# Retention and two MLP layers: the first 256-token units of the first layer begin one pair later, and the last unit follows the last pair

## The chip, the cores and the metric

The kernel runs on one core of one Trainium2 chip. The metric is the device time of one execution in microseconds (us), lower is better.

## What is computed

The reference makes a retention layer (attention without softmax, with a decay by distance) for 4 batches, 8 heads, 576 tokens and 64 values per head, and sends its 2304 tokens of 512 values through two layers with 2048 hidden values each.

```python
rel = pos[:, None] - pos[None, :]
Dmat = np.where(rel >= 0, gamma[:, None, None] ** rel[None, :, :], 0.0)
ret = scores * Dmat[None, :, :, :]          # scores = q k^T / 8
x = np.matmul(ret, v)                        # heads side by side: 2304 x 512
h = x @ w_in;  x = np.maximum(0.01 * h, h) @ w_out      # first layer
h = x @ w_in2; x = (h - np.tanh(h)) @ w_out2            # second layer
```

## The kernel before

**Precision.** Products that must be precise are made of three TensorE matmuls each, on a high and a low part of both factors (`xh`, `xl`, and the two halves of each `w` slot). The weights come as 64-bit floats. Each piece (128 x 512) is narrowed and split on the chip in these steps: a load (L147, issued on SyncE's queue, SP), `begin` on ScalarE (L164), `clamp` (L170), `shift` (L175), `top` and `low` (both L181) on VectorE, and a split into its two parts, ScalarE (L253) and then GpSimd (L254).

**Pairs.** The retention goes through 16 pairs (batch, two heads), numbered 0 to 15 here. Iteration `i` of the loop loads pair `i + 2`, makes the scores of pair `i` on TensorE (L674), has GpSimd scale its q (L642, and the last 64 tokens in L652), has VectorE mask the scores (L697, L708), and then calls `pair_steps(i)`: the outputs of pair `i - 1` on TensorE (L755, L766), the states of pair `i` (L723 on TensorE, L731 on ScalarE, L733 on VectorE), and the result of pair `i - 1`, split into `xh` (L774, ScalarE) and `xl` (L775, VectorE). The loads of a pair are four transfers on SP (L627, L628, L634, L635). The `kv` tiles have three buffers, so the transfer L634 of pair `i + 2` waits until the outputs of pair `i - 1` have been read, and what stands behind it on SP waits too.

**Units.** From pair `first` on, each pair also holds a share of the first layer, a unit of 256 tokens and two of the first four hidden blocks; there are 12, numbered 0 to 11. `unit_h(u)` is 24 matmuls into the one PSUM tile `x_b` (L822), then two activations on ScalarE that read it and write it (L828, L829), and a subtraction on VectorE that reads it (L830). Only after L830 may the next unit write `x_b`. `unit_o(u)` is 48 matmuls (L847) and stands one pair after `unit_h(u)`; `unit_evac` brings its sum out (L864, L866, L867). Units 0 and 1 need pieces 0 and 1 in `unit_h` and pieces 2 and 3 in `unit_o`; units 2 and 3 need pieces 4 and 5, and then 6 and 7.

**The narrowing steps.** All steps of the pieces stand in one list, and `fill(i, part)` issues it up to an index, at three places in each pair: part 0 ahead of `unit_h`, part 1 behind it, part 2 at the pair's end. The index is that of the table `early`, or else a third of the way between two `marks`. Pieces 0 to 7 take steps 0 to 52. Steps 53 and 54 are the loads of the first two of eight *kept* pieces (output weights of the second layer, `in_w2o`), steps 55 and 56 are `begin` and `clamp` of the first one, steps 57 and 58 its `shift` and `top`. The pieces are loaded into unused columns of `acc`, in four places: a load also waits until the piece that lay there has been narrowed. From pair 9 on the index comes from `marks` alone: 57 for (9, 0), 59 for (9, 1), 62 for (9, 2).

All engines work through their instructions in the order in which the program issues them, and each waits for what it needs. After the retention the function `layers` goes on with the rest of both layers.

Of the kernel before, what the change touches and what calls it, by code (L numbers as in the profile page):

```python
# [35 lines left out]
def retention_moe_moe(  # L36
# [15 lines left out]
    B, NP, _, S = qT.shape  # L52
# [26 lines left out]
    def slot(k, lead):  # L79
        at = k * 1024 + (LEAD if lead else 0)  # L80
        return wide_all[:, at:at + 1024].rearrange("p (i c) -> p i c", i=2)
# [25 lines left out]
    for m in range(2):  # L107
        for g in range(NG):
# [13 lines left out]
            first = len(steps)  # L122
# [438 lines left out]
    def retention():  # L561
        with ExitStack() as ac:
# [208 lines left out]
            def finish(i, src, lo, hi):  # L771
# [13 lines left out]
            marks = [0] + at_pair + [  # L785
                base + 2 + (len(ops) - base - 2) * i // (len(order) - 8) for i in range(len(order) - 7)
            ]
            first = NP + 1
            done, u = [0], 0

            early = {
# [3 lines left out]
            }  # L795

            def fill(i, part):
# [11 lines left out]
            def place(u):  # L809
                half, block = u % 2, u // 2  # L810
                if u < SPLIT:
                    half, block = block, half
                return block * QW, half * 2

            def unit_h(u):
                t0, f0 = place(u)
                for f in range(2):
                    w = wt[0, 0, f0 + f]
                    for kk in range(KK):
                        cs = slice(kk * P, (kk + 1) * P)  # L820
                        for j, (wi, x) in enumerate(((0, xh), (0, xl), (1, xh))):
                            nc.tensor.matmul(  # L822
                                out=x_b[:, f, :], lhsT=w[:, wi, cs], rhs=x[:, kk, t0:t0 + QW],
                                start=f == 0 and kk == 0 and j == 0,
                                stop=f == 1 and kk == KK - 1 and j == 2, skip_group_check=True,
                            )
                gt = slot(N_OUT + u % 2, True).rearrange("p i (f n) -> p i f n", f=2)
                nc.scalar.activation(out=gt[:, 0], in_=x_b, func=AF.Prelu, alpha=0.01)  # L828
                nc.scalar.activation(out=x_b, in_=x_b, func=AF.Prelu, alpha=0.01)  # L829
                nc.vector.tensor_tensor(  # L830
                    out=gt[:, 1], in0=x_b, in1=gt[:, 0].bitcast(F32), op=ALU.subtract
                )
                gs[u] = gt

            def unit_o(u):
                t0, f0 = place(u)
                gt = gs.pop(u)
                alone = u < SPLIT
                if alone or f0 == 0:
                    accs[t0] = ps_a.tile([P, KK, QW], F32, tag="a", name="a")  # L840
                ps = accs[t0]
                for f in range(2):
                    w = wt[0, 1, f0 + f]
                    for d in range(KK):
                        for j, (wi, gi) in enumerate(((0, 0), (0, 1), (1, 0))):

                            nc.tensor.matmul(  # L847
                                out=ps[:, d, :], lhsT=w[:, wi, d * P:(d + 1) * P],
                                rhs=gt[:, gi, f, :],
                                start=(alone or f0 == 0) and f == 0 and j == 0 and d % 2 == 0,  # L850
                                stop=(alone or f0 > 0) and f == 1 and j == 2 and d % 2 == 1,
                                skip_group_check=True,
                            )

            def unit_evac(u):
                t0, f0 = place(u)
                if f0 == 0 and u >= SPLIT:
                    return
                ps = accs.pop(t0)
                dst = acc_t[:, :, t0:t0 + QW]  # L860
                if f0 and u < SPLIT:
                    for d in (0, 2):
                        part = dst[:, d:d + 2]
                        nc.vector.tensor_tensor(out=part, in0=ps[:, d:d + 2], in1=part, op=ALU.add)  # L864
                    return
                nc.scalar.activation(out=dst[:, 2:], in_=ps[:, 2:], func=AF.Copy)  # L866
                nc.vector.tensor_copy(out=dst[:, :2], in_=ps[:, :2])  # L867

            def pair_steps(i, fast):

                nonlocal u
                if fast:
                    unit_h(u)
                    fill(i, 1)
                    if u:
                        unit_o(u - 1)
                        unit_evac(u - 1)
                    u += 1
                if i:
                    ot = o_place(i - 1)  # L880
                    if i < GROUPED:
                        outputs_far(i - 1, ot, range(1, NFULL))
                        outputs_near(i - 1, ot, range(NFULL))
                        outputs_far(i - 1, ot, [NFULL])
                        outputs_near(i - 1, ot, [NFULL])
                    else:
                        outputs_far(i - 1, ot, range(1, NCH))
                        outputs_near(i - 1, ot, range(NCH))
                        finish(i - 1, ot[:, :MAIN], 0, MAIN)
                    del qk[i - 1]  # L890
                    del pts[i - 1], kv[i - 1]
                if i < len(order):
                    states_mm(i)
                    scores_tail(i)
                    states(i)
                if i:
                    finish(i - 1, x_t, MAIN, S)
                    if i < GROUPED:
                        finish(i - 1, ot[:, :MAIN], 0, MAIN)
                if i < len(order):  # L900
                    mask_tail(i)
                if i + 1 < GROUPED:
                    prep_tail(i + 1)
                if i + 1 < len(order):
                    prep_k(i + 1)
# [57 lines left out]
                    fill(i, 2)  # L963
            pair_steps(len(order), True)
            assert done[0] >= len(ops)
            unit_o(u - 1)
            unit_evac(u - 1)
            assert 2 * u == n_early
# [168 lines left out]
    with tc.manual_schedule():  # L1137
        retention()
        layers()
# [70 lines left out]
```

## Time and profile before

| | |
|---|---|
| median of 3 runs | 858.77 us (858.19 to 858.89) |
| profiled execution | 858.63 us |
| its span, first to last instruction | 856.7 us, so 1.93 us lie outside it |
| TensorE (PE) busy | 847.5 us (99%) |
| VectorE (DVE) busy | 608.5 us (71%) |
| ScalarE (ACT) busy | 445.7 us (52%) |
| GpSimd (POOL) busy | 377.7 us (44%) |

The span is the time from the first instruction to the last. A busy share says how long an engine had an instruction in work, and not whether the program waited for that engine; that is told by the waits and by the chain that ended last. PEld is TensorE's weight load. A name ending in q (SPq) is an engine's queue, its issuing side.

### The profile page before, as it was taken

To read this page: it belongs to the slowest core of one execution; us is meant where nothing else is said; L and a number is where in the kernel's file an instruction comes from. 1 tells how busy PE (TensorE), PEld (TensorE's weight loads), DVE (VectorE), ACT (ScalarE), POOL (GpSimd) and SP (SyncE) were. 2 spreads that over 40 slices of the span, in tenths; PEclk is the share of its full clock that TensorE was granted. 3 is DMA by queue.
4 is the path that set the end of the run, shared out by engine and by line. 5 is a ranking of instruction groups with operands and counts; after the bars stand their busy time and mean duration, and the time that the engine had idled before them with its cause. 6 is when DMAs were issued, how large, how long until landed. Compare 5 with 4: busy or idle time off the path is not lost.

```text
span 856.7 us, 15321 instructions
## 1 busy us (share of the span) xinstructions
PE 847.5 (99%) x5774; PEld 751.4 (88%) x5774; DVE 608.5 (71%) x1052; ACT 445.7 (52%) x879; POOL 377.7 (44%) x308
## 2 busy tenths in 40 slices
PE   9999999999999999999999999999999999999997
PEld 8889999888988888888888899888999899999996
DVE  7987875787675777658764687756766677677775
ACT  4453443453345334453544577765566566656663
POOL 4432322140146103363465487745445445544554
PEclk9999999999999999999999999999999999999999
DMA  9835755334365433645354512581225312563112
GB/s 346 320 121 186 240 158 189 103 110 137 124 219 204 143 123 103 241 177 158 158 199 151 192 63 86 173 343 74 75 99 205 140 74 75 204 238 124 50 50 73
DMA packets 37784, 133.77 MB, mean 156 GB/s; under 512 B 4304, under 2 KB 4944, under 8 KB 35664
## 3 DMA queue, kind: packets, MB, share of 16 engines
q1 hardware_dynamic: 37424, 132.66, 43.7%
q8 instruction: 45, 0.74, 0.3%
q14 instruction: 27, 0.22, 0.1%
q10 hardware_dynamic: 288, 0.15, 0.1%
HBM read 96.62 MB, written 36.18 MB: 155 GB/s over the span
## 4 chain that ended last, share of the span: by engine, by line
PE 93%; DVE 4%; issue 1%; ACT 1%; POOL 0%; DVEq 0%; POOLq 0%
PE a L426 41%; PE h L273 22%; PE h L307 18%; PE a L847 4%; PE x_b L822 3%; PE o L766 1%; PE sc L674 1%; DVE cw L181 1%; PE o L755 1%; PE x_c L723 1%; PE x_b L942 1%; DVE st L733 0%; DVE pt L697 0%; DVE xl L775 0%; PE x_e L687 0%
## 5 line engine op out<-in xcount | busy, mean ns | idle before, releaser
L426 PE MATMUL a<-w 128*128 128x512 f32 (+1 forms) x1680 | 394.3, 377 | 0.0
L426 PEld LDWEIGHTS a<-w 128*128 128x128 f32 x1680 | 293.4, 188 | 47.5
L254 POOL TENSOR_TENSOR w<-cw,w 128x512 fp32r<-128x512 f32 x80 | 113.6, 1438 | 240.1 <-ACT w L253 214.4
L273 PE MATMUL h<-xh,w 128*128 128x512 f32 (+1 forms) x672 | 186.9, 349 | 0.0
L366 POOL TENSOR_TENSOR v<-t,u 128x512 f32<-128x512 f32 (+1 forms) x76 | 93.5, 1230 | 98.2 <-ACT t L363 92.2
L273 PEld LDWEIGHTS h<-xh,w 128*128 128x128 f32 x672 | 119.4, 188 | 17.0
L398 POOL TENSOR_TENSOR w<-v,w 128x512 fp32r<-128x512 f32 (+1 forms) x76 | 96.3, 1267 | 62.2 <-ACT w L397 62.1
L352 ACT ACTIVATE w<-h 128x512 fp32r<-128x512 f32 (+1 forms) x68 | 37.2, 547 | 159.9 <-PE h L273 115.7
L273 PE MATMUL h<-xl,w 128*128 128x512 f32 (+1 forms) x336 | 117.0, 348 | 0.0
L307 PE MATMUL h<-xh,w 128*128 128x256 f32 x512 | 100.8, 281 | 0.2
L307 PEld LDWEIGHTS h<-xe,w 128*128 128x128 f32 x576 | 80.9, 189 | 9.5 <-DVE mk L301 1.8
L181 DVE SCALAR_TENSOR_TENSOR cw<-st,cw 128x512 uint32<-128x512 uint32 x96 | 86.5, 901 | 2.5
L392 DVE SCALAR_TENSOR_TENSOR v<-q,v 128x512 f32<-128x512 f32 (+1 forms) x76 | 61.9, 814 | 36.5 <-POOL v L366 35.4
L307 PEld LDWEIGHTS h<-xh,w 128*128 128x128 f32 x512 | 83.1, 190 | 2.8 <-DVE v L395 1.5
L307 PE MATMUL h<-xe,w 128*128 128x256 f32 x576 | 84.2, 282 | 0.4 <-DVE mk L301 0.4
L511 DVE TENSOR_TENSOR acc<-a,acc 128x512 f32<-128x512 f32 (+1 forms) x113 | 71.3, 657 | 17.0 <-PE a L426 17.0
L362 ACT ACTIVATE u<-h 128x512 f32<-128x512 f32 (+1 forms) x80 | 44.2, 553 | 73.5 <-DVE h L301 51.3
L397 ACT ACTIVATE w<-v 128x512 fp32r<-128x512 f32 (+1 forms) x76 | 45.3, 596 | 62.5 <-DVE v L395 60.0
L170 DVE TENSOR_SCALAR cw<-cw 128x512 f32<-128x512 f32 x64 | 33.6, 525 | 55.6 <-ACT cw L164 55.4
L307 PE MATMUL h<-xl,w 128*128 128x256 f32 x256 | 71.8, 280 | 0.0
L273 PEld LDWEIGHTS h<-xl,w 128*128 128x128 f32 x336 | 63.3, 188 | 8.6
L253 ACT ACTIVATE w<-cw 128x512 fp32r<-128x512 f32 x80 | 47.0, 621 | 31.6 <-DVE cw L181 17.8
(95 smaller groups left out, 1178.4 us busy)
## 6 DMA issues: line engine op xcount, KB each, us to landing
kept<-w SPq DMA_DIRECT2D x48, 512.0 KB, 3.4
w<-kept SPq DMA_DIRECT2D x48, 512.0 KB, 4.7
xe<-xkept SPq DMA_DIRECT2D x12, 1536.0 KB, 6.5
st<-in_w2i SPq DMA_DIRECT2D x16, 512.0 KB, 4.1
st<-in_w1i SPq DMA_DIRECT2D x12, 512.0 KB, 4.4
st<-in_w1o SPq DMA_DIRECT2D x12, 512.0 KB, 3.5
xkept<-xe SPq DMA_DIRECT2D x4, 1536.0 KB, 8.8
kv<-in_vn SPq DMA_DIRECT2D x16, 320.0 KB, 3.3
```

What stands on the lines that cost most here:

```text
L181: nc.vector.scalar_tensor_tensor(out=t["w"], in0=t[src], scalar=scalar, in1=t["w"], op0=op, op1=ALU.bitwise_or)
L253: nc.scalar.activation(out=wp[:, 0, :], in_=wf, func=AF.Copy)
L254: nc.gpsimd.tensor_tensor(out=wp[:, 1, :], in0=wf, in1=wp[:, 0, :].bitcast(F32), op=ALU.subtract)
L273: nc.tensor.matmul(out=ps[:, :n], lhsT=w[:, wi, cs], rhs=x[:, kk, t0:t0 + n], start=kk == 0 and i == 0, stop=kk == KK - 1 and i == 2,)
L307: nc.tensor.matmul(out=out_, lhsT=w[:, wi_, at:at + P], rhs=x(xi, kk), start=start and kk == 0 and j == 0, stop=stop and kk == 1 and j == ...
L362: nc.scalar.activation(out=u[:, :n], in_=h, func=AF.Square)
L366: nc.gpsimd.tensor_tensor(out=v[:, :n], in0=t_[:, :n], in1=u[:, :n], op=ALU.mult)
L392: nc.vector.scalar_tensor_tensor(out=v, in0=q, scalar=RHO_A, in1=v, op0=ALU.add, op1=ALU.mult)
L397: nc.scalar.activation(out=gt[:, 0, g_at(s)], in_=v, func=AF.Copy)
L398: (nc.gpsimd if m else nc.vector).tensor_tensor(out=gt[:, 1, g_at(s)], in0=v, in1=gt[:, 0, g_at(s)].bitcast(F32), op=ALU.subtract)
L426: nc.tensor.matmul(out=o, lhsT=l, rhs=r, start=f == 0 and i == 0 and d % pack == 0, stop=f == GF - 1 and i == 2 and (d + 1) % pack == 0, s ...
L511: nc.vector.tensor_tensor(out=dst, in0=a, in1=dst, op=ALU.add)
```

## The change

The first unit stands in pair 6 instead of pair 5 (`first = NP + 2`, with `NP` = 4). Eleven units then stand in pairs 6 to 15 and in the closing `pair_steps`, and the twelfth is written behind them: `unit_h(11)`, `unit_o(10)`, and then `unit_o(11)` as before. The table `early` has the steps 0 to 52 one pair later from pair 4 on, with other places in between.

```diff
-            first = NP + 1
+            first = NP + 2
             done, u = [0], 0
 
             early = {
-                (1, 0): 3, (2, 0): 6, (2, 2): 7, (3, 0): 11, (4, 0): 12, (4, 2): 20,
-                (5, 0): 24, (5, 1): 30, (5, 2): 34, (6, 0): 38, (6, 1): 44, (6, 2): 47,
-                (7, 0): 50, (7, 1): 51, (7, 2): 53,
+                (1, 0): 3, (2, 0): 6, (2, 2): 7, (3, 0): 11, (4, 0): 12, (4, 2): 14,
+                (5, 0): 17, (6, 0): 20, (6, 1): 27, (6, 2): 31, (7, 0): 34, (7, 1): 40,
+                (7, 2): 44, (8, 0): 46, (8, 1): 50, (8, 2): 53,
             }
...
             pair_steps(len(order), True)
             assert done[0] >= len(ops)
+            unit_h(u)
+            unit_o(u - 1)
+            unit_evac(u - 1)
+            u += 1
             unit_o(u - 1)
             unit_evac(u - 1)
```

On VectorE, from the mask of pair 5 on, the order before has piece 2 narrowed ahead of that mask (L170, L175 and two L181, then L697), and unit 0's subtraction (L830) behind the first half of piece 3:

```order
L170 TENSOR_SCALAR cw<-cw 128x512
L175 TENSOR_SCALAR cw<-cw 128x512
L181 SCALAR_TENSOR_TENSOR cw<-acc,cw 128x512 x2
L697 TENSOR_TENSOR pt_97<-sc,cm_sb 128x512 x2
L170 TENSOR_SCALAR cw<-cw 128x512
L175 TENSOR_SCALAR cw<-cw 128x512
L830 TENSOR_TENSOR w<-x_b,w 128x512
L181 SCALAR_TENSOR_TENSOR cw<-acc,cw 128x512 x2
```

In the change, from the same place, the mask of pair 5 comes first, the rest of pair 5 and the mask of pair 6 stand inside piece 2, and unit 0's subtraction stands behind piece 2:

```order
L697 TENSOR_TENSOR pt_97<-sc,cm_sb 128x512 x2
L170 TENSOR_SCALAR cw<-cw 128x512
L175 TENSOR_SCALAR cw<-cw 128x512
L775 TENSOR_TENSOR xl<-o,xh 128x512
L733 SCALAR_TENSOR_TENSOR st_94<-st_94,decay,x_c 128x64 x3
L775 TENSOR_TENSOR xl<-x_e,xh 128x64
L708 TENSOR_TENSOR pt_97<-x_e,cm_sb 64x64
L708 TENSOR_TENSOR pt_97<-x_c,cm_sb 64x64
L697 TENSOR_TENSOR pt_96<-sc,cm_sb 128x512 x2
L181 SCALAR_TENSOR_TENSOR cw<-acc,cw 128x512 x2
L830 TENSOR_TENSOR w<-x_b,w 128x512
```

So a whole pair's work on VectorE has moved ahead of each piece from piece 2 on, beside the one unit that stands a pair later.

On SP, a piece of the difference shows the loads of the first kept pieces (`in_w2o`). Before, two of them stand behind the loads of pair 10 and ahead of those of pair 11; in the change the loads of pair 11 come first, and three stand together behind them:

```order
-L147 DMA acc<-in_w2o 128x512 x2
+L147 DMA acc<-in_w1o 128x512
 L627 DMA qk<-in_qT 128x576
 L628 DMA qk<-in_kT 128x576
 L634 DMA kv<-in_kn 128x512
 L635 DMA kv<-in_vn 128x640
-L147 DMA acc<-in_w2o 128x512
+L627 DMA qk<-in_qT 128x576
+L628 DMA qk<-in_kT 128x576
+L634 DMA kv<-in_kn 128x512
+L635 DMA kv<-in_vn 128x640
+L147 DMA acc<-in_w2o 128x512 x3
```

The two loads have moved behind one more L634, that of pair 11, from pair 8 into pair 9.

On ScalarE, the order before has `begin` of the first kept piece (the L164 of these rows) in pair 9, behind the activations of unit 3 and ahead of those of unit 4:

```order
L828 ACTIVATE w<-x_b 128x512
L829 ACTIVATE x_b<-x_b 128x512
L774 ACTIVATE xh<-o 128x512
L731 ACTIVATE st_93<-x_c 128x64
L774 ACTIVATE xh<-x_e 128x64
L658 ACTIVATE kv<-kv,acc 128x4x64 x2
L164 ACTIVATE cw<-acc 128x512
L828 ACTIVATE w<-x_b 128x512
L829 ACTIVATE x_b<-x_b 128x512
```

In the change it is in pair 9 too, behind the split of piece 7 and ahead of the activations of unit 3:

```order
L253 ACTIVATE w<-cw 128x512
L164 ACTIVATE cw<-acc 128x512
L828 ACTIVATE w<-x_b 128x512
L829 ACTIVATE x_b<-x_b 128x512
L774 ACTIVATE xh<-o 128x512
L731 ACTIVATE st_94<-x_c 128x64
L774 ACTIVATE xh<-x_e 128x64
```

So the step that reads the kept piece has kept its pair, and its load stands in that same pair now instead of the one before.

## Rows read from the trace of the kernel before

**Rows 1.** The page: chain that ended last, shares of the span by engine.
```profile
PE 93%; DVE 4%; issue 1%; ACT 1%; POOL 0%; DVEq 0%; POOLq 0%
```

**Rows 2.** TensorE's waits, 0 to 170 us: us in total, times, longest.
```profile
PE x_b L822 <- POOL w L254: 1.9, 2, 1.1
```

**Rows 3.** TensorE by stretch: length, busy (instructions), granted clock, DMA share, GB/s.
```profile
5.13:7.14 2.01, 2.01 (x17) 1.00 0.90 318
9.40:10.49 1.09, 1.09 (x17) 1.00 1.02 417
...
28.55:33.15 4.60, 3.50 (x26) 1.00 0.96 337
46.94:51.33 4.39, 3.42 (x26) 1.00 0.66 251
...
67.76:70.59 2.83, 2.83 (x26) 1.00 0.96 313
```

**Rows 4.** TensorE in order of time: start, us, instruction [idle before <- releaser].
```profile
33.15 0.87 PE L755 MATMUL o<-qk,st 64*64 64x128 f32 x12
...
37.46 0.38 PE L822 MATMUL x_b<-xh,w 128*128 128x256 f32 x1 [0.40 <-DVE w L830]
```

**Rows 5.** VectorE in order of time, 49 to 55 us.
```profile
49.77 0.68 DVE L775 TENSOR_TENSOR xl<-o,xh 128x512 fp32r<-128x512 f32 x1
...
51.82 1.42 DVE L181 SCALAR_TENSOR_TENSOR cw<-acc,cw 128x512 uint32<-128x512 uint32 x2
53.27 1.29 DVE L697 TENSOR_TENSOR pt<-sc,cm_sb 128x512 f32<-128x512 f32 x2
54.48 1.06 DVE L170 TENSOR_SCALAR cw<-cw 128x512 f32<-128x512 f32 x1
```

**Rows 6.** VectorE by stretch: length, busy (instructions), granted clock, DMA share, GB/s.
```profile
25.00:60.00 35.00, 33.59 (x67) 1.00 0.62 217
```

**Rows 7.** VectorE in order of time, 48 us: an L170 while GpSimd is idle.
```profile
47.90 0.42 DVE L170 TENSOR_SCALAR cw<-cw 128x512 f32<-128x512 f32 x1
```

**Rows 8.** GpSimd in order of time: splits of pieces 6 and 7.
```profile
53.98 1.27 POOL L254 TENSOR_TENSOR w<-cw,w 128x512 fp32r<-128x512 f32 x1 [2.44 <-ACT w L253]
...
61.20 1.30 POOL L254 TENSOR_TENSOR w<-cw,w 128x512 fp32r<-128x512 f32 x1 [3.57 <-ACT w L253]
```

**Rows 9.** SP's waits, 0 to 120 us: us in total, times, longest.
```profile
SPq L634 <- PE x_e L766: 63.5, 13, 9.4
```

**Rows 10.** TensorE in order of time: pair 7's outputs end; units 4 and 5 begin.
```profile
65.77 0.28 PE L766 MATMUL x_e<-pt,kv 128*64 128x64 f32 x4
...
67.76 0.38 PE L822 MATMUL x_b<-xh,w 128*128 128x256 f32 x1
...
77.24 0.38 PE L822 MATMUL x_b<-xh,w 128*128 128x256 f32 x1
```

**Rows 11.** SP's queue in order of time, 66 to 68 us.
```profile
67.05 0.85 SPq L147 DMA_DIRECT2D acc<-in_w2o  x2
```

**Rows 12.** ScalarE in order of time, 72 us: `begin` of the first kept piece.
```profile
72.20 0.67 ACT L164 ACTIVATE cw<-acc 128x512 f32<-128x512 f32 x1 [4.08 <-DMA acc<-in_w2o]
```

**Rows 13.** VectorE in order of time, 74 us: unit 4's subtraction.
```profile
73.87 0.69 DVE L830 TENSOR_TENSOR w<-x_b,w 128x512 fp32r<-128x512 f32 x1 [0.54 <-ACT x_b L829]
```

**Rows 14.** Line L147, 0 to 100 us: issue to landing of its 13 loads.
```profile
DMA to landing us min/median/max: 3.5/6.0/7.1
```

**Rows 15.** Line L942, TensorE's first matmuls: weight loads, ns min/median/max.
```profile
L942 PEld LDWEIGHTS x_b<-pt x24: 192/333/333, 1.4 to 8.1; 128*128 128x128 f32 x24
```

**Rows 16.** TensorE in order of time, end of the retention: last two `unit_o`, then `layers`.
```profile
136.10 2.88 PE L847 MATMUL a<-w 128*128 128x256 f32 x24
...
140.97 3.10 PE L847 MATMUL a<-w 128*128 128x256 f32 x24
143.90 0.29 PE L273 MATMUL h<-xh,w 128*128 128x256 f32 x1
```

**Rows 17.** ScalarE in order of time, end of the retention: last split ahead of the last evacuations.
```profile
141.34 0.63 ACT L253 ACTIVATE w<-cw 128x512 fp32r<-128x512 f32 x1 [3.41 <-DVE cw L181]
```

## The prediction

> **What bounds the kernel now.** I read the chain that ended last first: TensorE holds 93% of it [rows 1], so the time is TensorE's work plus what TensorE waits. The change leaves its 12 units and 16 pairs as they are, so its work stays, and only waits can move the time. The list of TensorE's waits [rows 2] shows where they lie: in the first 170 us, behind the start, the units' matmuls L822 waited twice for a GpSimd split (1.9 us); once more one waited for VectorE's L830 (0.40 us, [rows 4]). The view by stretch gives these waits their full size, since matmuls beside a wait are stretched too: an undisturbed `unit_h` takes 2.83 us, that of unit 0 took 4.60 and that of unit 2 took 4.39 [rows 3]. That is 1.77 + 1.56 + 0.40 = 3.73 us in all. Behind unit 2 the units pay next to nothing, so 3.7 us (0.43%) is all that this stage has to give.
>
> **First part: the units' start, one pair later.** In pair 5 TensorE now has a pair's retention work alone, and every unit up to the tenth begins a pair's work later. A pair without its unit takes TensorE 37.46 - 0.40 - 33.15 = 3.91 us [rows 4]. But VectorE, which makes the pieces, has a pair more ahead of each piece too: L775, L733, L775 and two L708 from 49.77 to 51.82, and the mask from 53.27 to 54.48 [rows 5], 2.05 + 1.21 = 3.26 us. From 25 to 60 us VectorE is busy for 33.59 of 35 us [rows 6], so it is VectorE that sets when a piece is ready: before, piece 7 was split at 61.20 + 1.30 = 62.50 [rows 8]. The units come 3.91 later and the pieces 3.26 later, so of the 3.73 us only 0.65 comes back: **-0.65 us**. The waits go to other places (unit 0 free, unit 2 and perhaps `unit_o(2)` longer); the sum is what counts. Two bounds. If VectorE meets GpSimd less often, all 3.73 come back. An L170 that ran into a GpSimd split (53.98) took 1.06 instead of 0.42 us [rows 5, 7, 8], 0.64 each; three more such meetings, which the new places of the steps allow, turn -0.65 into +1.3. I take -0.65, as the six pieces meet GpSimd's work now as well. Pieces 5 and 6 are loaded behind pair 8's L634, 1.0 us after the outputs of pair 5; at the median landing of 6.0 us [rows 14] `begin` of piece 5 could run 7.0 us after these outputs, while its place on ScalarE comes up after states and scores (1.71), `unit_h(1)` (2.83) and two activations (some 1.1), 5.6 us. The 1.4 us between are hidden: two L181 and L830 (1.42 + 0.69 [rows 5, 13]) stand ahead of its `clamp` on VectorE. I cost that at nothing; without this cover it is 1.4 us.
>
> **Second part: the load of the first kept piece.** Steps 53 and 54 were issued in pair 8, because the table had 53 behind pair 7. Now the table has 53 behind pair 8, and `fill(9, 0)`, unchanged at 57, issues both loads and also `begin` and `clamp` of the same piece. On SP the loads stand behind pair 11's L634 instead of pair 10's. That L634 waits until the outputs of pair 8 are read: these waits are the largest that SP has, 13 of them [rows 9]. Before, the same thing can be read a pair earlier. The outputs of pair 7 ended at 65.77 + 0.28 = 66.05 [rows 10], the two loads went at 67.05 behind L634 [rows 11], ScalarE waited 4.08 us for the first and began L164 at 72.20 [rows 12]. Behind it stood unit 4's activations and L830, which ended at 73.87 + 0.69 = 74.56 [rows 13]. So `x_b` was free 8.51 us after the outputs. That cost nothing, since all this stood in pair 9 and the next unit began at 77.24 [rows 10]: 2.7 us of cover.
>
> In the change the whole chain begins a pair later, at the end of pair 8's outputs, inside pair 9, while `begin` stays in pair 9, now ahead of unit 3's activations in ScalarE's strict order. Behind the outputs TensorE has the states and the scores of pair 10, and wants `x_b` for unit 4 after 67.76 - 66.05 = 1.71 us [rows 10]. It gets it after 8.51. The wait is 8.51 - 1.71 = **+6.80 us**, once: with unit 4 the pairs have their old distance again, and the second piece, loaded at the same time, is wanted later. Behind the blocked L164 on ScalarE stand unit 3's activations, the result of pair 8 and the states of pair 9; VectorE waits for them with its `clamp`; TensorE waits for VectorE alone. The third load of the group waits for the first piece's place and holds pair 12's loads on SP, which are wanted two pairs later. Bounds: the 13 loads landed 3.5 to 7.1 us after their issue [rows 14] against 5.15 here, so the wait lies between 5.15 and 8.75 us. I take the one row that has the same queue ahead of it.
>
> **What the wait leaves behind.** No wait of TensorE in this trace is that long, but the start shows what it does after idling: nothing ran until 1.4 us, then its weight loads took 333 ns at the median against 192 at the fastest [rows 15], and the 16 score matmuls of pair 0 took 2.01 us where those of pair 1 took 1.09 [rows 3]. The granted clock reads 1.00, the 2.4 GHz level, in both stretches, so that column does not tell them apart; the pace does. From 1.4 to at least 7.14 us TensorE ran slow: 5.7 us at 1.09/2.01 of its pace lose 0.46 x 5.7 = 2.6 us. I take the same after the wait, **+2.6 us**; the bounds are 0 (the pace holds) and 3.2 (slow for 7 us). One place in the trace shows it and the column speaks against it, so I put the spell at five in seven. The page "TensorE: Matmul & The Clock Gate" of the Trainium skill, Part 1: The HAM clock gate, says that the array's clock is halved by default and again after idling, that sustained work lifts it, and that the records of it are not to be relied on for trn2. By that rule the spell comes and the sum stands at 867.4; if only the granted clock's column counted it would be 864.8.
>
> **Third part: the last unit behind the last pair.** `unit_h(11)` and `unit_o(10)` move behind the outputs of pair 15, same matmuls. `unit_h(11)` needs `x_b`, which unit 10 gives back under a `unit_o` and the outputs (136.10 to 140.97 before [rows 16], 4.87 us, against 1.8 for two activations and L830: 74.56 - 72.20 less the 0.6 of L164 [rows 12, 13]). `unit_o(10)` needs the sum of unit 9 evacuated, which stands on ScalarE behind the last split: before, that ended at 141.34 + 0.63 = 141.97 [rows 17], 5.87 us after its unit, plus as much as the split itself, 0.6, for the evacuation; now 4.87 + 2.83 = 7.70 us are there. `unit_o(11)` has `unit_o(10)` (2.9 us) ahead of it to cover unit 11's activations and L830 (1.8). **0 us**; if the first cover were gone, 1.0 us would show. `layers` begins without a wait now (143.90, [rows 16]) and has more time for its first weights after it, so nothing is gained there either.
>
> **Sum.** 858.63 (profiled execution: span 856.7 and 1.93 around it; the median is 0.14 higher) - 0.65 + 6.80 + 2.6 + 0 = 867.4 us, 1.0% slower.
>
> **Rivals.** *The wait without the slow spell*: 864.8 us. For it: the granted clock never left 1.00; against it: the start's pace. *Longer early waits*: three more meetings with GpSimd and the cover at the end or of piece 5 gone, +1.3 + 1.0 instead of -0.65, 870.3. *Faster*: the kept piece is there in time, because SP reaches its load before pair 8's outputs are done (the place in `acc` is free once piece 6 is narrowed), and the early waits fall away: 858.63 - 3.73 = 854.9. It decides at a wait of 3.7 us: `x_b` came free 74.56 - 72.20 = 2.36 us behind the landing, so the load would have to land 1.71 + 3.73 - 2.36 = 3.1 us after the outputs, 2.1 us after its issue, and the shortest of 13 took 3.5; or SP would have to pass L634 without its wait, and it waited there 13 times. *No change*: the load in time as there, the early waits only moved, -0.65: 858.0.
>
> **How the numbers follow.** Forecast 0.60, wait without slow spell 0.24, longer early waits 0.05: 0.89 slower. Faster 0.06. No change 0.05; a difference within 0.2% (1.7 us) can hardly be told from none here. For the range I take 862.5 (no slow spell, the load landing 2 us sooner or the early waits gone for the most part) to 869.5 (slow spell, the load landing 2 us later); that leaves out the faster and equal cases, half of the longest, and little else.
>
> **What would show it.** Right: a wait of about 7 us of L822 for VectorE's L830 in pair 10, ScalarE's L164 idle some 5 us or more for `in_w2o` just ahead of unit 3's L828, weight loads longer than 192 ns behind it, `unit_h(0)` at 2.83 us, `unit_h(2)` over 4. Wrong: L164 without a wait there, or L822 in pair 10 without one; early waits in all under 2 us or over 5; a TensorE wait between the last outputs and `layers`.

## The result, and the profile after

The changed kernel takes 868.35 us at the median (867.30 to 869.05, 4 runs) against 858.83 (858.19 to 859.13, 4 runs): ratio 1.0111, 95% interval 1.0093 to 1.0128, so 1.1% slower. Its profiled execution took 867.3 us, with a span of 865.4. That is 8.67 us above the profiled execution before and the shortest of its four runs, so the sums below explain 8.7 us; the medians lie 9.5 apart.

The page of after gives the chain that ended last, by engine (the answer to [rows 1]; here and below, an answer is the same view, read from the trace of after):

```profile
PE 91%; DVE 4%; issue 2%; DMA 1%; POOL 1%; ACT 1%; SPq 0%; DVEq 0%; POOLq 0%; ACTq 0%
```

TensorE still holds it, but a DMA has come into it, with 1%. TensorE's waits of after from 0 to 180 us say where (total, times, longest; the answer to [rows 2]):

```profile
PE x_b L822 <- DVE w L830: 7.0, 1, 7.0
...
PE x_b L822 <- ACT w L253: 1.0, 1, 1.0
PE x_b L822 <- POOL w L254: 0.8, 1, 0.8
...
PE a L847 <- POOL w L254: 0.5, 1, 0.5
PE x_e L755 <- DVE pt L713: 0.4, 1, 0.4
```

One wait of 7.0 us is new. The others shown are the early waits, in other places than before and about as large (2.7 us here, 1.9 + 0.4 before); the 0.4 us for L713 is a wait for a pair's mask, not for a piece. TensorE of after in order of time, around the long wait and at the end of the retention (the answers to [rows 10, 16]):

```profile
68.97 0.28 PE L766 MATMUL x_e<-pt,kv 128*64 128x64 f32 x4
...
69.92 1.11 PE L674 MATMUL sc<-qk 64*128 64x128 f32 x16
78.06 0.58 PE L822 MATMUL x_b<-xh,w 128*128 128x256 f32 x1 [7.03 <-DVE w L830]
...
83.18 2.99 PE L847 MATMUL a<-w 128*128 128x256 f32 x24
...
89.94 0.38 PE L822 MATMUL x_b<-xh,w 128*128 128x256 f32 x1
...
152.47 0.28 PE L273 MATMUL h<-xh,w 128*128 128x256 f32 x1
```

Unit 4 wanted `x_b` 1.71 us after the outputs of pair 8 had ended at 69.25, at 70.96, and began at 78.06: 7.10 us late. The next views show what it waited for. SP's queue of after in order of time (the answer to [rows 11]), with the L634 of pair 11 ahead of the two loads:

```profile
69.37 0.33 SPq L634 DMA_DIRECT2D kv<-in_kn  x1
69.74 0.43 SPq L635 DMA_DIRECT2D kv<-in_vn  x1
70.69 0.80 SPq L147 DMA_DIRECT2D acc<-in_w2o  x2
```

ScalarE of after (the answer to [rows 12]):

```profile
75.65 0.66 ACT L164 ACTIVATE cw<-acc 128x512 f32<-128x512 f32 x1 [11.32 <-DMA acc<-in_w2o]
76.22 0.58 ACT L828 ACTIVATE w<-x_b 128x512 fp32r<-128x512 f32 x1
76.69 0.59 ACT L829 ACTIVATE x_b<-x_b 128x512 f32<-128x512 f32 x1
```

VectorE of after (the answer to [rows 13]):

```profile
77.32 0.69 DVE L830 TENSOR_TENSOR w<-x_b,w 128x512 fp32r<-128x512 f32 x1 [0.54 <-ACT x_b L829]
```

SP's waits of after from 60 to 90 us (the answer to [rows 9]) name the outputs as what L634 waited for; the longest of its two waits, 8.5 us, ends at 69.37:

```profile
SPq L634 <- PE x_e L766: 12.4, 2, 8.5
```

Read as one chain: the outputs end at 69.25, L634 is free at 69.37, the loads go at 70.69, L164 starts at 75.65, unit 3's activations stand behind it, L830 ends at 78.01, and L822 starts at 78.06. ScalarE had nothing to do for 11.32 us, although `x_b` lay there ready to be read.

TensorE of after by stretch (length, busy (instructions), granted clock, DMA share, GB/s; the answer to [rows 3]):

```profile
32.40:35.30 2.90, 2.90 (x26) 1.00 1.02 365
48.60:54.00 5.40, 3.57 (x26) 1.00 0.88 294
...
71.00:73.00 2.00, 0.03 (x2) 0.93 0.94 305
73.00:75.00 2.00, 0.00 (x0) 0.50 0.91 336
...
78.06:83.18 5.12, 5.12 (x24) 0.52 0.00 0
83.20:86.10 2.90, 2.90 (x26) 1.00 0.64 212
```

Unit 0 runs undisturbed now (2.90 us), and unit 2 waits longer (5.40). In the long wait the granted clock falls to 0.50 (0.93 over its first 2 us), from the 2.4 GHz level to that of 1.2 GHz, and the 24 matmuls of unit 4 run almost wholly at it: 5.12 us instead of 2.83 [rows 3]. The next 24 have the full clock again.

The four parts add up: scores of pair 1 began 0.58 us earlier (8.82 against 9.40, see the last section), the wait is 7.10, and unit 4 lost 5.12 - 2.83 = 2.29. Unit 5 began at 89.94 instead of 77.24; less the 3.91 us of the pair that now stands ahead of it, that is 8.79 us later. So the early waits changed by 8.79 + 0.58 - 7.10 - 2.29 = -0.02 us. Behind unit 5 only 0.1 us was won (the span is 8.7 us longer).

### The profile page after: what moved, and what is told of

Same layout as the page of the kernel before. It is cut to its first block, busy times and chain, and to the rows that moved or that the text cites. A ratio compares the mean times of both kernels' runs of the same rounds, so it can differ in the third digit from the quotient of the medians.

```text
span 865.4 us, 15316 instructions
## 1 busy us (share of the span) xinstructions
PE 848.4 (98%) x5774; PEld 752.8 (87%) x5774; DVE 608.9 (70%) x1052; ACT 445.6 (51%) x879; POOL 377.3 (44%) x308
## 4 chain that ended last, share of the span: by engine, by line
PE 91%; DVE 4%; issue 2%; DMA 1%; POOL 1%; ACT 1%; SPq 0%; DVEq 0%; POOLq 0%; ACTq 0%
PE a L426 41%; PE h L273 22%; PE h L307 18%; PE x_b L822 3%; PE a L847 3%; PE o L766 1%; PE o L755 1%; PE sc L674 1%; DVE cw L181 1%; DMA qk<-in_kT 1%; DVE pt L697 1%; DMA acc<-in_w2o 1%; PE x_c L723 0%; DVE st L733 0%; POOL w L254 0%
## 5 line engine op out<-in xcount | busy, mean ns | idle before, releaser
L181 DVE SCALAR_TENSOR_TENSOR cw<-st,cw 128x512 uint32<-128x512 uint32 x96 | 86.5, 901 | 2.5
L170 DVE TENSOR_SCALAR cw<-cw 128x512 f32<-128x512 f32 x64 | 32.8, 512 | 64.1 <-ACT cw L164 63.9
L381 DVE TENSOR_TENSOR h<-h,t 128x512 f32<-128x512 f32 (+1 forms) x80 | 51.3, 642 | 14.6 <-ACT t L363 14.5
```

The lines of the kernel that those rows point to most:

```text
L181: nc.vector.scalar_tensor_tensor(out=t["w"], in0=t[src], scalar=scalar, in1=t["w"], op0=op, op1=ALU.bitwise_or)
L381: nc.vector.tensor_tensor(out=h, in0=h, in1=tmp[s][1][:, :n], op=ALU.subtract)
```

## Experiments

Each kernel was timed beside the kernel before on the same chip, whose median was 858.40, 858.39 and 858.48 us in the three groups. The first four are about the load of the first kept piece.

**The load alone put back** (the change, with the index for (8, 2) at 55 instead of 53):

```diff
-                (7, 2): 44, (8, 0): 46, (8, 1): 50, (8, 2): 53,
+                (7, 2): 44, (8, 0): 46, (8, 1): 50, (8, 2): 55,
```

> The changed kernel with the index of (8, 2) set from 53 to 55, so that the loads of the first two kept pieces are issued in pair 8 again, ahead of pair 11's loads on SP; nothing else moves. Theory (the late load makes the whole loss): no wait of L822 for L830 in pair 10, unit_h(4) back to about 2.83 us, and the time back by 7.0 + 2.3 us to some 859.0, since the early waits of the changed kernel sum to about 0.2 us more than before. Rival A (the units' new places cost by themselves): 861 or more, with waits elsewhere. Rival B (the -0.65 of the prediction's first part): 858.0.

Measured: 858.93 us (858.08 to 859.38), ratio 1.0005 (0.9996 to 1.0014). One number of the table takes back 868.35 - 858.93 = 9.4 us, as much as the wait and the slow unit of after together (7.10 + 2.29 = 9.39). SP and ScalarE of this kernel in order of time show why:

```profile
60.86 0.33 SPq L634 DMA_DIRECT2D kv<-in_kn  x1
...
61.77 3.43 SPq L147 DMA_DIRECT2D acc<-in_w2o  x2
```

```profile
66.80 0.67 ACT L164 ACTIVATE cw<-acc 128x512 f32<-128x512 f32 x1 [1.34 <-DMA acc<-in_w2o]
67.37 0.58 ACT L828 ACTIVATE w<-x_b 128x512 fp32r<-128x512 f32 x1
```

The loads now stand behind pair 10's L634, not pair 11's, and L164 waits 1.34 us under cover of a unit, instead of 11.32. What is left of the change, units one pair later and a unit at the end, is worth nothing that can be measured.

**The kernel before with its load made late** (its table, with nothing issued in pair 8):

```diff
-                (7, 0): 50, (7, 1): 51, (7, 2): 53,
+                (7, 0): 50, (7, 1): 51, (7, 2): 53, (8, 0): 53, (8, 1): 53, (8, 2): 53,
```

> The kernel before with the index held at 53 through pair 8, so that the two loads of kept pieces are issued in pair 9 and nothing else moves; its units stay where they were. Theory: the same wait appears without the rest of the change, about 7 us of L822 for L830 in pair 10 and then a unit_h of about 5.1 us at the lower clock level, 868 us (866.5 to 869.5). Rival (the wait needs the moved units): under 860.

Measured: 867.56 us (867.19 to 868.21), ratio 1.0108 (1.0094 to 1.0122). The old kernel gets the change's whole loss from this alone, with its units where they were. Its ScalarE in order of time, and TensorE by stretch:

```profile
81.39 0.66 ACT L164 ACTIVATE cw<-acc 128x512 f32<-128x512 f32 x1 [13.52 <-DMA acc<-in_w2o]
```

```profile
81.00:83.00 2.00, 0.00 (x0) 0.68 0.30 119
83.00:85.00 2.00, 1.20 (x5) 0.50 0.00 0
85.00:90.00 5.00, 5.00 (x32) 0.65 0.16 16
```

TensorE waited 6.7 us for L830 there, and the clock fell in the wait as in after.

**The late load left, its reader moved behind** (the change, with `begin` at the end of pair 9):

```diff
-                (7, 2): 44, (8, 0): 46, (8, 1): 50, (8, 2): 53,
+                (7, 2): 44, (8, 0): 46, (8, 1): 50, (8, 2): 53, (9, 0): 55, (9, 1): 55,
```

> The changed kernel with the index of (9, 0) and (9, 1) at 55: the loads stay in pair 9 behind pair 11's L634, and only begin, clamp, shift and top of the first kept piece move to the end of pair 9, behind unit 3's activations and the result of pair 8. Theory (what costs is the queue behind the blocked begin on ScalarE and VectorE, not the transfer): ScalarE still waits some 3 us or more for in_w2o, but x_b is free in time, and the mask of pair 10 on VectorE may come 0.4 us late; 859 to 860.5. Rival (the transfer itself, or the memory traffic beside it, holds TensorE): 866 or more.

Measured: 861.02 us (860.62 to 863.04), ratio 1.0036 (1.0022 to 1.0050), somewhat above the expectation. With the load as late as in the change, 7.3 of the 9.4 us come back once nothing of TensorE's stands behind the reader. So the loss needs both: a load behind L634, and its reader ahead of unit 3's activations in ScalarE's order. The rest is, for the most part, one pair later: this kernel's L164 still waited 4.29, 0.61 and 2.11 us for kept pieces, VectorE's narrowing came late behind it, and from 80 to 87 us TensorE waited three times, which its list of waits shows:

```profile
PE x_b L822 <- DVE w L830: 0.8, 1, 0.8
...
PE sc L674 <- PE x_c L687: 0.5, 1, 0.5
...
PE a L847 <- DVE acc L864: 0.2, 1, 0.2
```

The outputs behind these waits begin at 89.29, in the first experiment's kernel at 87.45: 1.8 us, as much as the two profiled executions differ (860.87 and 859.06).

**The late load on another queue** (the change, with these two loads issued by ScalarE, so that they pass no L634):

```diff
-            ops = piece_ops(pieces, ahead=3) + [lambda k=k: load_piece(k) for k in early_kept[:2]]
+            ops = piece_ops(pieces, ahead=3) + [lambda k=k: load_piece(k, nc.scalar) for k in early_kept[:2]]
```

> The changed kernel with the same two loads at the same place of the program, but issued on ScalarE's queue instead of SP's, so that they do not stand behind pair 11's L634. Theory (SP's order makes the load late): they are issued some 6 us sooner, right after the split of piece 7, the wait in pair 10 shrinks to under 2 us, no slow spell follows, 859 to 861. Rival (the load is late because it is issued in pair 9 at all, whatever the queue): 865 or more.

Measured: 859.15 us (858.46 to 860.29), ratio 1.0012 (1.0002 to 1.0021). Program order and reader are the change's; only the queue is another. This kernel's ScalarE in order of time:

```profile
64.43 0.82 ACTq L147 DMA_DIRECT2D acc<-in_w2o  x2
68.24 0.68 ACT L164 ACTIVATE cw<-acc 128x512 f32<-128x512 f32 x1 [3.24 <-DMA acc<-in_w2o]
```

The load goes at 64.43, without waiting for outputs, and the 3.24 us that ScalarE then waits are covered. So it is SP's order behind L634 that made the load late.

The next experiments are about the early waits, of which the prediction said that VectorE's piece-making sets them.

**Less work on VectorE** (the `clamp` of pieces 0 to 7 is left out, so this part of the narrowing isn't computed; in the first kernel of this section, and in the kernel before):

```diff
-        return [begin, clamp, shift, top, low]
+        return [begin, clamp if key[0] or key[2] >= GF else (lambda: None), shift, top, low]
```

> The changed kernel with the two loads in pair 8, and with the clamp (L170) of pieces 0 to 7 left out, so that values outside the range of 32-bit floats would be narrowed wrongly; all else the same. Theory (VectorE's chain sets the early waits): six clamps of 0.42 us or more fall out of the chain between pair 5 and piece 7, the early waits shrink by 2 to 3 us of some 4, 856.0 to 857.2. Rival (ScalarE's order or GpSimd sets them): less than 0.6 us gained, 858.2 or more.

> The kernel before with the clamp (L170) of pieces 0 to 7 left out, so that values outside the range of 32-bit floats would be narrowed wrongly; all else the same. Theory: the same gain of 2 to 3 us as in the changed kernel, 855.6 to 856.8, so that the units' place makes no difference with either chain. Rival: less than 0.6 us gained; or a gain much unlike that of the changed kernel, if the two kernels wait for different things.

Measured: 855.81 us (ratio 0.9972, 0.9961 to 0.9983) and 856.16 us (0.9975, 0.9964 to 0.9985). Taking some 5 us of VectorE's time away (8 L170, 5.3 us in before) won 3.1 us on the one (0.2 below the range that I gave) and 2.2 on the other. Some 0.6 of the 3.1 go with the granted clock: seven of the eleven executions of the first kernel read 0.997 at the mean, while these read 0.999 or 1.00, and against its other four (858.08 to 858.51) the gain is some 2.5 us. The pieces are what unit 2 waits for, and VectorE's work sets them, with the units early or late.

**The same work on another engine** (the first kernel of this section, with that `clamp` on GpSimd; everything is computed):

```diff
+            eng = nc.vector if key[0] or key[2] >= GF else nc.gpsimd
-            nc.vector.tensor_scalar(
+            eng.tensor_scalar(
```

> The change with the load in pair 8, and the clamp of pieces 0 to 7 issued on GpSimd instead of VectorE; everything is still computed. Theory: the pieces come from ScalarE, VectorE and GpSimd in turn, and GpSimd's work slows VectorE's beside it (1.06 us instead of 0.42 for the same L170 before), so the clamp on GpSimd takes the piece at least as long as on VectorE: 858 to 861 us, no gain. Rival: VectorE's occupied time alone sets the pieces, GpSimd has room (under half busy), and the gain is that of leaving the clamp out: about 856 us.

Measured: 862.64 us (862.27 to 865.23), ratio 1.0053 (1.0039 to 1.0067): no gain, and 1.6 us above the range that I gave. GpSimd and VectorE of this kernel, 12 to 70 us, by line (one line further down in it: L171 is `clamp`, L176 `shift`; busy us, mean ns, idle before):

```profile
L171 POOL TENSOR_SCALAR cw<-cw 128x512 f32<-128x512 f32 x8 | 16.2, 2026 | 6.3 <-ACT cw L164 6.0 <-DMA qk<-in_qT 0.3
...
L176 DVE TENSOR_SCALAR cw<-cw 128x512 uint32<-128x512 uint32 x8 | 8.1, 1012 | 6.8 <-POOL cw L171 6.8
```

The clamp takes 2026 ns on GpSimd, and VectorE stood still for 6.8 us behind it; its `shift` also took longer, 1012 ns against 850 in the first kernel of this section. The profiled execution is the longest of the five (865.23 us), so these rows show the kind of loss and not its size at the median. The latency of a piece through its engines in turn counts, not VectorE's busy time alone.

**The units late, the steps early** (the change, with the table of before):

> The changed kernel with the table early of the kernel before: the units one pair later, the narrowing as early as before (and so the loads of kept pieces in pair 8). Theory (VectorE's chain sets the early waits, wherever units and steps stand): VectorE has the same instructions ahead of pair 9's scores, TensorE then waits for masks of pairs instead of split pieces, early waits in all 4 to 5 us as in the other kernels, no wait for in_w2o ahead of a unit's activations; 858.5 to 860. Rival (the units' weights are late because the new table narrows late): early waits under 1.5 us, 856 or less.

Measured: 864.52 us (863.47 to 865.95), ratio 1.0074 (1.0059 to 1.0089): my expectation was wrong by 4.5 us or more. The pieces do come in time (no unit waits for one), but pair work of VectorE's is late instead. This kernel's VectorE, and then its TensorE, in order of time:

```profile
30.37 3.31 DVE L181 SCALAR_TENSOR_TENSOR cw<-acc,cw 128x512 uint32<-128x512 uint32 x2
33.71 1.29 DVE L697 TENSOR_TENSOR pt<-sc,cm_sb 128x512 f32<-128x512 f32 x2
```

```profile
35.10 1.25 PE L674 MATMUL sc<-qk 64*128 64x128 f32 x11 [3.24 <-issue]
```

The profile names no releaser ("issue"), but the scores start 0.1 us after the masks L697 have read the scores before them, and these stood behind narrowing. The same thing came again at 45.49. Its list of waits gives 5.1 us for these two, and the clock reads 0.50 in 36 to 38 and in 46 to 48 us. So masks instead of pieces, and some 5 us of waits, were as expected; what the expectation left out is the clock behind them. The two blocks of scores and the two `unit_h` that follow took 1.68, 1.98, 3.93 and 3.62 us, 3.4 more than at 1.09 and 2.83. In the kernel before, a unit stood there, and TensorE had work while VectorE narrowed. So the later units needed a later table than that of before: with the steps of that table as early as they were, the pair work was not in time.

**The units two pairs later** (the first kernel of this section, with `first = NP + 3` and two units behind the last pair):

> The change with the load in pair 8 (first experiment), and the units one pair later still: first = NP + 3, the table as it is, two units behind the last pair. Theory: VectorE sets when a piece is ready, and the steps stay in their places, so the pieces come no later and the units 3.9 us later: the early waits of about 4 us go, but the pair that now has no unit gives VectorE's narrowing no cover, and TensorE waits there for masks or states instead, as with the old table; the sum lies within 1.5 us of the first experiment, 857.5 to 860.5 us. Rival: the early waits are the units' alone and the free pair costs nothing: 855 to 856 us, as without the clamp.

Measured: 860.20 us (858.98 to 861.27), ratio 1.0020 (1.0011 to 1.0029). Another 3.9 us of lead for every piece won nothing. TensorE of this kernel in order of time shows the waits in new places:

```profile
43.78 1.16 PE L674 MATMUL sc<-qk 64*128 64x128 f32 x16 [0.90 <-PE x_c L687]
46.73 0.38 PE L822 MATMUL x_b<-xh,w 128*128 128x256 f32 x1 [1.79 <-DVE w L830]
...
57.02 0.39 PE L822 MATMUL x_b<-xh,w 128*128 128x256 f32 x1 [0.72 <-DVE w L830]
```

The units no longer wait for pieces but for L830, the subtraction of the unit before them, which now stands behind narrowing on VectorE. The first of these rows is again a wait for masks: VectorE's L697 ended at 43.68. So the early waits moved once more, as the expectation had it.

**The last unit alone behind the last pair** (the kernel before, with its last unit moved):

```diff
-            pair_steps(len(order), True)
+            pair_steps(len(order), False)
+            unit_h(u)
+            fill(len(order), 1)
...
+            unit_o(u - 1)
+            unit_evac(u - 1)
+            u += 1
```

> The kernel before with its last unit alone moved behind pair 15's outputs, as in the change (unit_h(11) and then both last unit_o); the units' start and the table stay. Theory (nothing waits there): no wait of TensorE between the last outputs and the layers but for up to 0.3 us, 858.2 to 859.2. Rival (a wait for the last unit's activations or for the evacuated sum): 860 or more.

Measured: 860.55 us (859.88 to 860.97), ratio 1.0023 (1.0014 to 1.0032), 2.2 us above before where I expected almost nothing. It is not quite the change's end: here no unit stands ahead of the last outputs, and its TensorE waits there, in order of time:

```profile
133.22 0.89 PE L755 MATMUL o<-qk,st 64*64 64x128 f32 x12 [0.56 <-ACT xh L774]
134.46 0.33 PE L755 MATMUL x_e<-qk,st 64*64 64x64 f32 x4 [0.35 <-DVE pt L708]
...
144.14 0.28 PE L273 MATMUL h<-xh,w 128*128 128x256 f32 x1
```

But `layers` begins only 0.24 us later than before (143.90, [rows 16]), and the other 0.96 us of the longer span lie behind that, in `layers`: there its list of waits has 1.1 us, against 0.4 in the kernel before. Why, these runs do not show, and the profiled execution (859.88) is the shortest of the ten. So this experiment doesn't price the change's own end. Neither after nor the first kernel of this section has a wait of TensorE from 138 to 180 us.

## Why the prediction was right

It said 867.4 us with a range of 862.5 to 869.5 and 1.0% slower; 868.35 was measured. By its steps:

**The late load, +6.80 us, was right**: 7.10 us in after's trace. Its links were 1.44 us from the outputs' end to the load (1.00 before), 4.96 from there to L164 (5.15 before), and 2.41 from L164 to unit 4 (before, 2.36 from L164 to the end of L830): 8.81 less 1.71. That the chain is the cause is shown four times: taken away by the load's place in the table or by its queue, taken away for the most part by its reader's place, and brought back in the old kernel.

**The slow spell, +2.6 us, was right in kind**: 2.29 us. Of the two signs that the prediction weighed, the pace at the start and a column that read 1.00 there, the pace told the truth; in this wait the column shows the spell too, at 0.50. The page "TensorE: Matmul & The Clock Gate" of the Trainium skill, Part 1: The HAM clock gate, says that the array's clock is halved after idling and comes back with work; these rows (0.50 in the wait, 0.52 in unit 4, 1.00 behind it) agree. The weight loads of unit 4, one of the prediction's signs, took 320 and 328 ns at the mean (`xh` and `xl`), those of unit 5 188. The bare wait would have cost 7.1 us, and the first experiment took back 9.4. That the size fits is in part luck: it was read from the start of one execution, slow to at least 7.14 us; in after the start was back at its pace by 5.08, and the same sum would have given 0.46 x 3.7 = 1.7 us.

**The early waits, -0.65 us, are the step that was mis-sized**: they changed by -0.02 us in the trace. Up to the end of `unit_h(2)` the sum held. GpSimd's splits, of piece 5 before and of pieces 5 and 7 in after, in order of time:

```profile
48.72 1.27 POOL L254 TENSOR_TENSOR w<-cw,w 128x512 fp32r<-128x512 f32 x1 [3.41 <-ACT w L253]
```

```profile
51.42 1.27 POOL L254 TENSOR_TENSOR w<-cw,w 128x512 fp32r<-128x512 f32 x1 [2.02 <-ACT w L253]
...
64.41 1.28 POOL L254 TENSOR_TENSOR w<-cw,w 128x512 fp32r<-128x512 f32 x1 [4.22 <-ACT w L253]
```

Counted from the scores of pair 1 (9.40 and 8.82), piece 5 came 52.69 - 49.99 + 0.58 = 3.28 us later, where the prediction had 3.26, and `unit_h(2)` ended 54.00 - 51.33 + 0.58 = 3.25 later: 0.66 won against 3.91. Piece 7 came 65.69 - 62.50 + 0.58 = 3.77 later, and `unit_o(2)`, which needs it, waited 0.5 us where it had not waited before. The prediction named that wait ("perhaps") and gave it no price. That the waits only go to other places was right: unit 0 free, unit 2 at 5.40 us instead of 4.39, that 0.5 us, and 0.4 us of TensorE in pair 5, which has no unit now, for VectorE's L713. The experiments bear out the reason behind it, VectorE: less work there gains 2.2 to 3.1 us, while more lead for the units gains nothing. Not foreseen in the prediction was that VectorE's other work pays at once when the narrowing keeps its place: TensorE waited for masks with the old table, and for L830 with units still later.

**The end, 0 us, was right in the trace**: no TensorE wait there, and from unit 5 to the first matmul of `layers` after took 152.47 - 89.94 + 3.91 = 66.44 us against 66.66. The experiment that was to confirm it by itself did not, as told.

That the sum of 867.4 us comes within 0.1 us of the profiled execution (867.3) is luck: the early waits came out 0.63 above it and the long wait 0.30, the spell 0.31 below, and the start, for which the sum has no term, 0.58 below. The median lies 0.95 above the forecast.

The first kernel of the experiments sums up the rest: without the late load, what the change is otherwise made of leaves the time where it was. The rival "no change" had that mechanism, and the late load decided against it. No version that computes everything was faster than before.

## What to carry to other kernels

When steps are moved later, look at each load among them for what now stands ahead of it on its queue: a transfer that waits for a buffer makes the load behind it as late as the engine that frees the buffer. Then look at what stands behind its reader: here a kept piece that nobody needed for a long time held up the activations that TensorE needed in 2 us. And a long TensorE wait can cost more than its length: here 7.10 us of waiting cost 2.29 more, as the 24 matmuls behind it ran at the lower clock.

## What the runs showed of the hardware

The start's slow pace is not the same in every execution, and the granted clock does not show it. The 16 score matmuls of pair 0 took 2.01 us before [rows 3], but 1.09 us in after, where both read 1.00; TensorE of after in order of time (the block of 16, and the next instruction):

```profile
5.08 1.16 PE L674 MATMUL sc<-qk 64*128 64x128 f32 x16 [0.18 <-DMA qk<-in_kT]
6.17 1.16 PE L942 MATMUL x_b<-pt 128*128 128x128 f32 x8
```

With it the pairs began 0.58 us earlier, which is as large as the early term of the prediction and hides it in a comparison of two spans.

The clock can fall behind short waits as well. In the profiled execution of the first experiment's kernel (859.06 us) TensorE had the two waits of unit 2 that after has too (0.97 and 0.85 us), and then ran at the lower level; TensorE by stretch:

```profile
48.70:53.80 5.10, 3.28 (x25) 1.00 0.92 294
53.90:57.90 4.00, 4.00 (x23) 0.58 0.06 24
```

In after, 50 to 58 us read 1.00 throughout. Such a spell, some 4.0 x 0.42 = 1.7 us here, can be there in one execution and missing in another. Not all of it stays: the outputs of pair 8 ended at 70.39 here and at 69.25 in after, and unit 2 had begun 0.17 later (48.77 and 48.60), so some 1.0 us is left; after's 0.5 us wait in `unit_o(2)` is gone here. The mean granted clock of every execution goes with it: the eleven of this kernel read 0.997 in seven (858.79 to 859.38 us) and 0.999 or 1.00 in four (858.08 to 858.51), and the four of after 0.992 in the two longest (868.84 and 869.05) and 0.994 in the others (867.30 and 867.85). That it is such a spell that spreads the four runs of after over 1.75 us, and lifts their median above the profiled execution, fits these numbers, but only one execution of each kernel was traced.
